# The low halves of a weight matrix: a subtraction on VectorE replaced by a negated copy on ScalarE and an adding DMA asked for by GpSimd

## The chip, the cores and the metric

The kernel runs on one core of a Trainium2 chip. The metric is the time of the device in microseconds (us), lower is better; a kernel is run several times and its median stands. Engines are called PE (TensorE, the matrix engine), DVE (VectorE), ACT (ScalarE), POOL (GpSimd) and SP (SyncE, which here only asks for DMAs).

## What is computed

Attention over 4 batches, 8 heads, 576 tokens and 64 dimensions a head, with a threshold on the scores; then two feed-forward networks over the 2304 tokens (model width 512). The change touches the first matrix of the second network, `w_in` of `_moe2_ref`, 512 by 2048:

```python
def _moe2_ref(x, w_in, w_out):
    h = x @ w_in
    g = np.maximum(h, 0.0) + np.log1p(np.exp(-np.abs(h)))
    return (g @ w_out).astype(np.float32)
```

The inputs are float64 for the weights and float32 for q, k, v. The products are made with pairs of float32r halves (below), so that they come close to float32.

## The kernel before, in words

**Products from halves.** A float32 value w is held as a high half, w rounded to float32r, and a low half, w minus the high half. A product of two such values takes three matmuls: high by high, high by low, low by high. So each weight matrix must be split before PE can use it, and `convert` does that.

**Stages.** The attention comes first, with units of the first network (`m1_unit`, 256 tokens each) between its heads. When the attention's buffers are closed (`close_at`), the weights of the second network are loaded and split while PE works on the last units of the first network, and the second network follows: token blocks 0, 1 and 4 as plain products, blocks 2 and 3 together by a scheme that trades products for sums.

**The split of w_in.** The matrix is loaded in 16 chunks of 128 by 512 float64 words (`prep_w2`), 512 KB each, into two rotating buffers of the tag `raw2`. Per chunk, `convert` issues: `a1` on ACT (the upper words, line 620), `a2` on DVE (the lower words shifted, line 621), `a4` on DVE (both joined to a float32 word, line 623), `a5` on ACT (rounded, the high half `w2h`, line 634) and a subtraction on DVE (the low half `w2l`, line 636). The buffer is free for the next load but one when the last of them is done. The same function splits the other matrices; its path for w_out of the second network (`raw_out`, `wo2h`, `wo2l`) is the same one.

**What reads it.** Block 0 of the second network (`m2_products`, line 809) multiplies chunk after chunk with the tokens in `x2m0h` and `x2m0l`, which SP loads from DRAM (`m2_load`, line 420). Its first product stands in the middle of the last units of the first network: their two matrix products (lines 697 and 751/752) and their transposes (line 734) share PE with it. Later blocks use the same halves again.

**What sets the order.** Each engine runs a list of operations that is written out by hand, `TURNS`, a table of operation numbers for each engine; negative numbers on PE are fillers, that many small matmuls on the identity (line 413), each in two passes in the trace. The costs that stand beside each `op(...)` served to make that table. An engine executes its list strictly in order, so a wait at the head holds everything behind it; SP asks for nearly all DMAs, in one list. POOL makes the identity at the start and then has nothing to do.

Of the kernel before, what the change touches and what calls it, by code (L numbers as in the profile page):

```python
# [9 lines left out]
F32 = mybir.dt.float32  # L10
F32R = mybir.dt.float32r
U32 = mybir.dt.uint32
# [58 lines left out]
def took(rows, row):  # L71
# [48 lines left out]
    "DVE":  # L120
# [267 lines left out]
def plan_of(nc, ctx, sb, const, ident, minus, pools, stacks, w1t, x2s, sums2, q, k, v, tau, w_in, w_out, g_ln, w2_in, w2_out, out):  # L388
# [221 lines left out]
    def convert(name, raw, hi, lo, n, after, view=lambda x: x, scale=None, turned=False):  # L610
# [3 lines left out]
        def lw():  # L614
            return view(raw.t[:, :, 0])

        def hw():
            return view(raw.t[:, :, 1])
# [525 lines left out]
```

## Time and profile before

| | before |
|---|---|
| time, median of 3 runs | 902.43 us (901.03 to 902.45) |
| the profiled execution's own time | 899.62 us |
| its span in the trace | 897.8 us |
| PE busy | 882.8 us, 98% |
| DVE busy | 722.0 us, 80% |
| ACT busy | 604.0 us, 67% |
| POOL busy | 0.7 us |
| DMA, share of 16 engines (hardware queue of SP) | 30.2%, 89.56 MB |

The time of an execution is a little longer than the span of its recorded instructions: here by 1.8 us. A busy PE is not PE at its peak, since matmuls overlap in the records; idle time of PE is what can be read from such a table, and what an engine off the path does with its idle time costs nothing by itself. All times in the sections below are of the profiled execution, counted from the start of its span.

### The profile page before, as it was taken

How to read it: one execution, taken by the hardware profiler on the slowest of the kernel's cores; microseconds unless marked ns; L12 is line 12 of the kernel's file. 1: busy time of each engine (PE TensorE's matmuls, PEld its weight loads, DVE VectorE, ACT ScalarE, POOL GpSimd, SP SyncE). 2: the span in 40 equal slices, each digit the busy share in tenths (PEclk: the TensorE clock that was granted, in tenths of full speed). 3: DMA queues.
4: the chain of work that ended last, by engine and by line, in shares of the span. 5: the costliest groups of instructions: out<-in, count | busy, mean ns of one | idle time of the engine just before them, and what ended most of it. 6: DMA issues, size and time to landing. Idle time of an engine off the chain costs nothing.

```text
span 897.8 us, 14490 instructions
## 1 busy us (share of the span) xinstructions
PE 882.8 (98%) x5348; PEld 693.9 (77%) x5348; DVE 722.0 (80%) x1558; ACT 604.0 (67%) x1189; POOL 0.7 (0%) x6
## 2 busy tenths in 40 slices
PE   7899999999999999999999999999999999999997
PEld 5567666777677777888888888888888988888886
DVE  5888988868878878778777979888998968999832
ACT  5989977887877788666666766755654645666521
POOL 0000000000000000000000000000000000000000
PEclk9999999999999999999999999999999999999999
DMA  8422300121113100083324444234337543212001
GB/s 278 171 94 57 106 7 1 56 85 54 46 53 89 42 13 2 24 279 132 106 95 141 164 134 169 99 127 152 120 133 236 181 164 129 70 71 71 34 15 47
DMA packets 46086, 90.86 MB, mean 101 GB/s; under 512 B 4800, under 2 KB 22720, under 8 KB 46016
## 3 DMA queue, kind: packets, MB, share of 16 engines
q1 hardware_dynamic: 45696, 89.56, 30.2%
q8 instruction: 42, 0.69, 0.3%
q10 hardware_dynamic: 320, 0.38, 0.2%
q14 instruction: 28, 0.23, 0.1%
HBM read 62.13 MB, written 27.79 MB: 100 GB/s over the span
## 4 chain that ended last, share of the span: by engine, by line
PE 93%; DVE 3%; ACT 2%; DMA 1%; issue 0%; SPq 0%; POOLq 0%; POOL 0%; ACTq 0%; DVEq 0%
PE w L842 21%; PE h L809 12%; PE w L697 11%; PE w L504 8%; PE s L528 8%; PE w L563 7%; PE w L751 7%; PE w L752 4%; PE h_b L1060 4%; PE h_a L1060 2%; PE h_g L1060 2%; PE w L734 2%; PE w L604 1%; PE s L583 1%; DVE nm L485 1%; PE w L542 1%
## 5 line engine op out<-in xcount | busy, mean ns | idle before, releaser
L485 DVE TENSOR_REDUCE nm<-s 128x1 f32<-128x576 f32 x144 | 103.2, 752 | 40.7 <-PE s L528 34.9
L842 PE MATMUL w<-wo2h,gh 128*128 128x512 f32 x288 | 112.3, 390 | 0.0
L842 PE MATMUL w<-wo2l,gh 128*128 128x512 f32 x288 | 112.3, 390 | 0.0
L842 PE MATMUL w<-wo2h,gl 128*128 128x512 f32 x288 | 112.0, 389 | 0.0
L486 ACT ACTIVATE E<-s,nm 128x576 f32<-128x576 f32 x128 | 92.6, 749 | 24.3 <-DVE nm L485 23.0
L488 DVE SCALAR_TENSOR_TENSOR E<-E,etau 128x576 f32<-128x576 f32 x128 | 101.9, 812 | 7.7 <-ACT E L486 5.3
L507 ACT COPY eT<-w 128x512 f32<-128x512 f32 (+1 forms) x186 | 94.2, 546 | 20.2 <-PE w L504 19.3
L751 PE MATMUL w<-lhl,wo1h 128*128 128x512 f32 x288 | 104.2, 401 | 0.0
L528 PE MATMUL s<-k,q 64*128 64x288 f32 x512 | 81.7, 429 | 3.5 <-ACT E L486 3.2
L504 PE MATMUL w<-ident,E 128*128 128x128 f32 x576 | 81.4, 280 | 1.7 <-ACT eT L507 0.9
L504 PEld LDWEIGHTS w<-ident,E 128*128 128x128 f32 x576 | 62.7, 140 | 24.4 <-ACT eT L507 7.3
L752 PE MATMUL w<-lhl,wo1l 128*128 128x256 f32 x288 | 80.6, 280 | 0.0
L563 PE MATMUL w<-eT,v 128*64 128x256 f32 (+1 forms) x680 | 76.3, 371 | 0.2
L528 PEld LDWEIGHTS s<-k,q 64*128 64x128 f32 x512 | 45.7, 186 | 26.1 <-ACT E L486 8.2
L563 PEld LDWEIGHTS w<-eT,v 128*64 128x64 f32 x680 | 44.7, 137 | 26.3 <-ACT eT L507 5.6
L751 PEld LDWEIGHTS w<-lhl,wo1h 128*128 128x128 f32 x288 | 54.1, 188 | 12.6 <-issue 0.4
L842 PEld LDWEIGHTS w<-wo2h,gl 128*128 128x128 f32 x288 | 54.1, 188 | 11.5
L842 PEld LDWEIGHTS w<-wo2h,gh 128*128 128x128 f32 x288 | 54.2, 188 | 10.1
L842 PEld LDWEIGHTS w<-wo2l,gh 128*128 128x128 f32 x288 | 54.2, 188 | 10.0
L697 PE MATMUL w<-w1h,xh 128*128 128x512 f32 x144 | 59.7, 415 | 0.0
L697 PE MATMUL w<-w1h,xl 128*128 128x512 f32 x144 | 56.5, 393 | 0.0
L697 PE MATMUL w<-w1l,xh 128*128 128x512 f32 x144 | 56.3, 391 | 0.0
(162 smaller groups left out, 1827.7 us busy)
## 6 DMA issues: line engine op xcount, KB each, us to landing
x2s<-x SPq DMA_DIRECT2D x36, 256.0 KB, 2.1
raw_in<-in_w_in_dram SPq DMA_DIRECT2D x16, 512.0 KB, 3.7
raw_out<-in_w_out_dram SPq DMA_DIRECT2D x16, 512.0 KB, 3.6
wsum<-g_w SPq DMA_DIRECT2D x16, 512.0 KB, 3.3
sw<-wsum SPq DMA_DIRECT2D x16, 512.0 KB, 3.7
v<-in_v_dram SPq DMA_DIRECT2D x16, 320.0 KB, 3.8
q<-in_q_dram SPq DMA_DIRECT2D x30, 144.0 KB, 3.2
raw<-in_w_out_dram SPq DMA_DIRECT2D x4, 1024.0 KB, 6.1
```

Source lines behind the costliest of these rows:

```text
L485: mx = op("DVE", 668, 750, lambda: dve.tensor_reduce(out=nm.t, in_=src(), axis=AX.XY, op=ALU.max, negate=True), after=[after], takes=[nm], ...
L486: ex = op("ACT", 638, 741, lambda: act.activation(out=dst().rearrange("p (a b) -> p a b", a=2), in_=src(), func=AF.Exp, bias=nm.t, scale=1.0),
L488: return op("DVE", 739, 900, lambda: dve.scalar_tensor_tensor(out=dst(), in0=dst(), scalar=etau, in1=dst(), op0=ALU.is_ge, op1=ALU.mult, a ...
L504: pe.transpose(bk.t[:, P * i:P * i + P], b_.t[:, c:c + P], ident)
L507: copies.append(op("ACT", occ, occ + 111, lambda: act.copy(out=eT.t[:, 0:width], in_=bk.t[:, 0:width]), after=[g], uses=[bk, eT]))
L528: pe.matmul(s[h].t[:, nh, 0:288], z["q"].t[r, c:c + P], z["k"].t[r, 288 * nh:288 * nh + 288], start=True, stop=True)
L563: pe.matmul(o_.t[64 * h:64 * h + 64, 0:W], z["v"].t[:, vcols(c, h)], e[8 if c == 8 else 4 * h + c](), start=(i == 0), stop=(i == 4))
L697: pe.matmul(ps.t, x__[:, part, :], w_[:, part, 512 * n:512 * n + 512], start=(part == 0 and j_ == 0), stop=(part == 3 and j_ == 2))
L751: pe.matmul(o.t.rearrange("p (a q) -> p a q", a=2), w1t["wo1h"][:, c, P * m:P * m + P], lhl.t[:, :, c, :], start=(c == 0), stop=False)
L752: pe.matmul(o.t[:, 0:256], w1t["wo1l"][:, c, P * m:P * m + P], lhl.t[:, 0, c, :], start=False, stop=(c == 7))
L809: pe.matmul(ps.t[:, 0:n], w2t["in", a, c][:, part, :], x(b_)[:, part, 0:n], start=(part == 0 and j_ == 0), stop=(part == 3 and j_ == 2))
L842: pe.matmul(ys[j].t, g_.t[:, P * j:P * j + P], w2t["out", a, c], start=(first and i == 0), stop=(last and i == 2))
```

## The change

For the 16 chunks of w_in alone (names that begin with `w2in`), the joined float32 words are written packed into the first half of the raw buffer, no longer into every second word; ACT writes minus the rounded words into the low half (`neg`, line 637 of the changed kernel), beside the high half as before; and a DMA that POOL asks for adds the float32 words of the raw buffer onto the low half, in place (line 638). The subtraction on DVE is gone. Readers of a low half now wait for that DMA, and so does the load that takes the raw buffer next. The table `TURNS` is written anew for all engines.

```diff
-        w_ = lambda: lw().bitcast(F32)
+        packed = name.startswith("w2in")
+        w_ = (lambda: raw.t.rearrange("p n t -> p (n t)")[:, 0:n].bitcast(F32)) if packed else lambda: lw().bitcast(F32)
...
-        a4 = op("DVE", 70 + 1068 * k_, 150 + 1070 * k_, lambda: dve.scalar_tensor_tensor(out=lw(), in0=hw(), scalar=3, in1=lw(), op0=ALU.logical_shift_left, op1=ALU.bitwise_or), after=[a1, a2], uses=[raw])
+        a4 = op("DVE", 70 + 1068 * k_, 150 + 1070 * k_, lambda: dve.scalar_tensor_tensor(out=w_().bitcast(U32), in0=hw(), scalar=3, in1=lw(), op0=ALU.logical_shift_left, op1=ALU.bitwise_or), after=[a1, a2], uses=[raw])
...
         a5 = op("ACT", 90 + 930 * k_, 200 + 940 * k_, lambda: act.copy(out=hi(), in_=w_()), after=[last], uses=[raw])
+        if packed:
+            neg = op("ACT", 90 + 930 * k_, 200 + 940 * k_, lambda: act.activation(out=lo(), in_=w_(), func=AF.Copy, scale=-1.0), after=[last], uses=[raw])
+            return [a5, op("POOL", 1100, None, lambda: pool.dma_start(out=lo(), in_=w_(), accum_op=ALU.add), after=[neg], uses=[raw], kb=2 * took(128, 4 * n))]
         if not turned:
             return [op("DVE", 70 + 1067 * k_, 150 + 1070 * k_, lambda: dve.tensor_tensor(out=lo(), in0=w_(), in1=f(hi()), op=ALU.subtract), after=[a5], uses=[raw])]
```

The table's row for POOL:

```diff
     "POOL":
-        "0",
+        "0 2303 2310 2317 2324 2331 2338 2352 2345 2359 2366 2373 2380 2387 2394 2401 2408",
```

**Order on SP** where the attention ends: `raw_in` are the loads of the chunks of w_in, `x2m0h` and `x2m0l` the loads of block 0's tokens (each in two parts), `x2s` the stores of the first network's results. Before:

```order
L420 DMA raw_in0_4644<-in_w2_in_dram 128x1024
L420 DMA raw_in1_4656<-in_w2_in_dram 128x1024
L420 DMA x2m0l_4662<-x2s0_87 128x4x256
L420 DMA x2s2_89<-x2_2_2_4423 128x512
L420 DMA x2m0l_4662<-x2s1_88 128x4x256
L420 DMA x2m0h_4674<-x2s0_87 128x4x256
L420 DMA raw_in2_4710<-in_w2_in_dram 128x1024
L420 DMA raw_in3_4734<-in_w2_in_dram 128x1024
L420 DMA x2m0h_4674<-x2s1_88 128x4x256
L420 DMA x2s3_90<-x2_3_0_4685 128x512
```

Now:

```order
L420 DMA raw_in0_4643<-in_w2_in_dram 128x1024
L420 DMA raw_in1_4647<-in_w2_in_dram 128x1024
L420 DMA x2m0h_4657<-x2s0_87 128x4x256
L420 DMA x2m0h_4657<-x2s1_88 128x4x256
L420 DMA x2s2_89<-x2_2_3_4437 128x512
L420 DMA x2s3_90<-x2_3_0_4650 128x512
L420 DMA raw_in2_4737<-in_w2_in_dram 128x1024
L420 DMA raw_in3_4749<-in_w2_in_dram 128x1024
L420 DMA x2m0l_4754<-x2s0_87 128x4x256
L420 DMA x2m0l_4754<-x2s1_88 128x4x256
```

Both parts of `x2m0l` have moved behind the loads of chunks 2 and 3; before, one part of `x2m0h` stood there.

**Order on ACT** at the same place, from the first step of chunk 0 to the first step of chunk 2 (in the changed kernel line 621 is `a1`, 635 the high half, 637 the negated copy; 700/704, 710/714, 754/758 and 758/762 are steps of the first network). Before:

```order
L620 ACTIVATE raw_in0_4644<-raw_in0_4644 128x512
L620 ACTIVATE raw_in1_4656<-raw_in1_4656 128x512
L634 CAST w2h0_4624<-raw_in0_4644 128x512
L700 COPY h4_1_4585<-w321_4584 128x512
L700 COPY h4_1_4585<-w322_4652 128x512
L634 CAST w2h1_4626<-raw_in1_4656 128x512
L754 COPY x2s_3_0_4730<-w315_4684 128x256
L710 ACTIVATE u4_1_4732,few4_1_4717<-h4_1_4585,few4_1_4717 128x1024
L758 CAST x2_3_0_4685<-x2s_3_0_4730 128x256
L620 ACTIVATE raw_in2_4710<-raw_in2_4710 128x512
```

Now:

```order
L621 ACTIVATE raw_in0_4643<-raw_in0_4643 128x512
L621 ACTIVATE raw_in1_4647<-raw_in1_4647 128x512
L637 ACTIVATE w2l0_4624<-raw_in0_4643 128x512
L635 CAST w2h0_4623<-raw_in0_4643 128x512
L637 ACTIVATE w2l1_4626<-raw_in1_4647 128x512
L758 COPY x2s_3_0_4705<-w315_4649 128x256
L704 COPY h4_1_4610<-w321_4609 128x512
L762 CAST x2_3_0_4650<-x2s_3_0_4705 128x256
L704 COPY h4_1_4610<-w322_4664 128x512
L635 CAST w2h1_4625<-raw_in1_4647 128x512
...
L621 ACTIVATE raw_in2_4737<-raw_in2_4737 128x512
```

The negated copies stand ahead of the high halves and ahead of the first network's steps.

**Order on PE** at block 0's first product, `h2_0_0` (line 809 before, 813 now); `w318` is the last group of sums of a unit of the first network, 16 matmuls in all. Before, its last rows and the product:

```order
L751 MATMUL w318_4826<-lhl3_4501,wo1h_85 128x512
L752 MATMUL w318_4826<-lhl3_4501,wo1l_86 128x256
L809 MATMUL h2_0_0_4854<-x2m0h_4674,w2h0_4624 128x512
L809 MATMUL h2_0_0_4854<-x2m0l_4662,w2h0_4624 128x512
L809 MATMUL h2_0_0_4854<-x2m0h_4674,w2l0_4625 128x512
```

Now:

```order
L701 MATMUL w332_4727<-w1h_83,xl5_0_4360 128x512
L813 MATMUL h2_0_0_4819<-x2m0h_4657,w2h0_4623 128x512
L813 MATMUL h2_0_0_4819<-x2m0l_4754,w2h0_4623 128x512
L813 MATMUL h2_0_0_4819<-x2m0h_4657,w2l0_4624 128x512
L755 MATMUL w318_4824<-lhl3_4495,wo1h_85 128x512
...
L813 MATMUL h2_0_1_4852<-x2m0h_4657,w2h1_4625 128x512
L813 MATMUL h2_0_1_4852<-x2m0l_4754,w2h1_4625 128x512
L813 MATMUL h2_0_1_4852<-x2m0h_4657,w2l1_4626 128x512
```

The first product has moved ahead of all 16 matmuls of `w318`, and the first product of chunk 1 now follows right behind them. No other operation has joined or left the work ahead of the first product. At the very start of PE's list the fillers are 15 (10 and 5) where they were 16 (15 and 1), and 2 further fillers some places later are gone.

## Rows read from the trace of the kernel before

**Rows 1.** The page: busy time of PE; its granted clock in 40 slices.

```profile
PE 882.8 (98%) x5348; PEld 693.9 (77%) x5348; DVE 722.0 (80%) x1558; ACT 604.0 (67%) x1189; POOL 0.7 (0%) x6
...
PEclk9999999999999999999999999999999999999999
```

**Rows 2.** Windows: start and end, length, then busy time of each engine.

```profile
core 0: us, PE busy (x) PEld busy (x) DVE busy (x) ACT busy (x) POOL busy (x), PEclk, DMA share, GB/s
0.00:36.00 36.00, 29.07 (x167) 19.66 (x168) 22.61 (x45) 26.30 (x46) 0.70 (x6) 1.00 0.86 279
36.00:380.00 344.00, 342.20 (x2706) 245.29 (x2706) 284.76 (x687) 279.80 (x567) 0.00 (x0) 1.00 0.16 48
380.00:525.00 145.00, 145.00 (x778) 122.64 (x775) 113.10 (x257) 94.59 (x199) 0.00 (x0) 1.00 0.44 151
640.00:700.00 60.00, 58.22 (x302) 49.79 (x301) 56.02 (x121) 32.02 (x65) 0.00 (x0) 1.00 0.56 183
```

**Rows 3.** Waits of PE, whole span: total us, times, longest.

```profile
PE s L528 <- ACT E L486: 3.2, 3, 1.6
PE h L809 <- DVE gw L826: 1.8, 1, 1.8
...
PE w L643 <- ACT eT L507: 1.2, 1, 1.2
```

**Rows 4.** Groups by line: the subtraction and the rounded copy of w_in's chunks.

```profile
L636 DVE TENSOR_TENSOR w2l<-raw_in,w2h 128x512 fp32r<-128x512 f32 x16 | 11.0, 686 | 1.0 <-ACT w2h L634 0.7
...
L634 ACT CAST w2h<-raw_in 128x512 fp32r<-128x512 f32 x16 | 10.5, 657 | 0.7 <-DVE raw_in L623 0.7
```

**Rows 5.** Timeline of the start: start us, duration us, engine, line, operation.

```profile
1.35 6.61 PE L413 MATMUL w<-ident 128*128 128x128 f32 x32 [1.35 <-POOL ident masks.py:199]
...
4.36 0.68 ACT L445 ACTIVATE k<-k 128x576 f32<-128x576 f32 x1 [1.10 <-DMA k<-in_k_dram]
...
7.89 1.24 PE L528 MATMUL s<-k,q 64*128 64x288 f32 x8
```

**Rows 6.** Timeline, SP alone, where the attention ends.

```profile
382.30 0.86 SPq L420 DMA_DIRECT2D raw_in<-in_w_in_dram  x2
...
389.69 2.38 SPq L420 DMA_DIRECT2D raw_in<-in_w_in_dram  x2
392.12 0.43 SPq L420 DMA_DIRECT2D x2m0h<-x2s  x1
```

**Rows 7.** Timeline: first steps of chunks 0 and 1 on ACT, joining of chunk 1 on DVE.

```profile
386.27 0.69 ACT L620 ACTIVATE raw_in<-raw_in 128x512 f32<-128x512 f32 x1 [2.48 <-DMA raw_in<-in_w_in_dram]
...
387.64 0.69 ACT L620 ACTIVATE raw_in<-raw_in 128x512 f32<-128x512 f32 x1 [0.68 <-DMA raw_in<-in_w_in_dram]
...
388.37 0.69 DVE L623 SCALAR_TENSOR_TENSOR raw_in<-raw_in 128x512 uint32<-128x512 uint32 x1 [0.29 <-ACT raw_in L620]
```

**Rows 8.** DMA issues by line: KB each, median us from issue to landing.

```profile
x2s<-x SPq DMA_DIRECT2D x36, 256.0 KB, 2.1
raw_in<-in_w_in_dram SPq DMA_DIRECT2D x16, 512.0 KB, 3.7
...
tsum<-g_x SPq DMA_DIRECT2D x12, 256.0 KB, 2.7
```

**Rows 9.** The tile x2m0h: time to landing of its two loads.

```profile
DMA to landing us min/median/max: 5.4/6.9/8.5
```

**Rows 10.** Timeline of PE: the first matmul of w318, and block 0's first product.

```profile
401.71 0.40 PE L751 MATMUL w<-lhl,wo1h 128*128 128x512 f32 x1
...
404.54 0.40 PE L809 MATMUL h<-x2m0h,w2h 128*128 128x512 f32 x1
```

**Rows 11.** Timeline around the longest later wait: ACT's wait, then PE's.

```profile
690.93 0.62 ACT L886 CAST g_w<-f_w 128x512 fp32r<-128x512 f32 x1 [3.13 <-DMA wsum<-g_w]
...
693.63 0.50 PE L809 MATMUL h<-x2m,w2h 128*128 128x256 f32 x2 [1.78 <-DVE gw L826]
```

**Rows 12.** Line 723: count, then duration ns min/median/max, first and last start.

```profile
L723 DVE TENSOR_SCALAR h<-u,few x18: 806/812/817, 109.2 to 506.1; 128x1024 f32<-128x1024 f32 x18
```

258 rows, old and new, of the table TURNS are left out of this document.

## The prediction

> **What bounds the kernel now.** Read the page first: PE is busy for 882.8 of 897.8 us, and its granted clock stays in the top tenth to the end [rows 1], which is the upper of its two levels, 2.4 GHz. So there is nothing to win from the clock, and at most 15.0 us from PE's idle time. Then ask where that idle time lies. The windows show it [rows 2]: 6.9 us of it in the first 36 us, 1.8 us between 36 and 380 us, 1.8 us between 640 and 700 us, and none at all between 380 and 525 us, the stretch in which the 16 chunks of w_in are split. There DVE works 113.1 and ACT 94.6 of 145 us; PE works all of it. The rest of the 15 us is the end of the span. PE's own waits tell what the idle time waited for [rows 3]: the largest is the start's loop of scores and softmax (3.2 us on ACT), the next a single wait of 1.8 us on DVE late in the second network. Neither is in the part that the change rewrites. The chain of work thus runs through PE's list from end to end, and a change pays only by what it does to that list and to the few waits at its head.
>
> **What goes.** 16 subtractions on DVE of 686 ns, 11.0 us in all [rows 4]. All are executed between 380 and 525 us, beside a PE without a gap: DVE falls there from 113.1 to about 102.1 of 145 us. Cover: PE's own work. Gain on the path: 0. The packed joining has as many elements as before, so I take `a4` at its old duration.
>
> **What comes on ACT.** 16 negated copies over the same 128x512 words as the rounded copy, 657 ns [rows 4]: 10.5 us, and ACT rises from 94.6 to about 105.1 of 145 us [rows 2]. Cover: again PE's work; ACT keeps 40 us of air in the stretch. On the path: 0, as long as ACT does not wait at the head of its list for a chunk that comes late, which is the next question.
>
> **What comes as a wait.** Each chunk now ends with an adding DMA, of which the trace shows no example. Call D the time from the end of the negated copy to its landing, POOL's asking included. It decides two things: when the low half can be read, and when the raw buffer is free for the next load but one. On POOL nothing stands behind it but the next such DMA.
>
> Bounds for D from the nearest rows [rows 8]: not under 2.1 us, the store of 256 KB, which reads and writes half of what the adding DMA reads; not over about 8.1 us, three passes of 256 KB one after another at 2.7 us. It reads 512 KB (source and destination), as many bytes as a raw load, 3.7 us, and writes 256 KB in addition. I take 4.5 us, between the raw load and two passes of 2.7 us.
>
> Follow chunks 0 and 1 in the changed order. Their loads start where they did, at 382.3 us [rows 6], since the attention's last matmul has kept its place but for one small exchange. ACT's first steps start at 386.3 and 387.6 us, and chunk 1 is joined by 388.37 + 0.69 = 389.1 us [rows 7]. On ACT follow the negated copy of chunk 0 (388.3 to 389.0), the rounded copy, and the negated copy of chunk 1 (389.6 to 390.3). The adding DMAs land at 389.0 + D and 390.3 + D: at 4.5 us, 393.5 and 394.8 us.
>
> *Readers.* Block 0's first product stood at 404.54 us and moves ahead of the 16 matmuls that began at 401.71 us [rows 10], to about 401.7 us: cover 8.2 us for low half 0. Chunk 1's first product comes 16 + 3 matmuls later, at about 405.2 us: cover 10.4 us. The other chunks' first products stand more than 120 groups of PE's work further on. No wait for a low half below D = 12.
>
> *The queue behind the buffer.* Here is the tight place. SP asks for the load of chunk 3 only once chunk 1's adding DMA has landed, and both loads of `x2m0l` are now queued behind it, where before only one load of `x2m0h` was. The first product needs `x2m0l`. The last of its two loads is asked for at about 390.3 + D + 0.9, three issues of some 0.4 us, as the one at 392.12 us took [rows 6]. Landing took 5.4 us for the load that stood in just this place, behind two raw loads, and 6.9 us in the median [rows 9]. So `x2m0l` is there at 396.6 + D to 398.1 + D, against PE's 401.7. PE waits nothing for D up to 5.1 (or 3.6) and one for one beyond. At 4.5 us: 0 to 0.9 us; I take 0.5.
>
> *ACT behind a late chunk.* The changed list puts 9 operations between the negated copy of chunk 1 and the first step of chunk 2. If chunk 2 lands late, ACT waits there; its 40 us of air and the free banks of PE's sums are the cover. I cost it at 0 for D near 4.5; without that cover each microsecond of D above costs one again at each pair of chunks.
>
> A page's price for D: the Trainium skill, "DMA: Bandwidth & Descriptors" (Anatomy of one DMA — SWDGE (gpsimd) path), gives a DMA asked for by GpSimd 2.0 us plus its bytes at 436 GB/s; for 512 KB that is an estimate of 3.2 us, and with it the wait for `x2m0l` would be 0 and the sum below -0.4. No row here shows such a DMA.
>
> **What is moved.** At the start one filler of 16 is gone, in the trace 2 of 32 passes: 6.61 / 32 = 0.21 us each [rows 5]. The first scores begin right behind the fillers, at 7.89 us, while k was scaled by 5.04 us, so the fillers hold them up: -0.4 us, if q has landed by 7.5. The 2 fillers further on stood in a gap: 0. The late wait of 1.8 us [rows 3] comes from ACT, which waits 3.13 us for a store of sums and holds DVE [rows 11]; the changed order on DVE still has that sum ahead of the operation that PE waits for, so I leave the wait where it is: 0, with bounds of -1.8 (gone) and +1.3 (ACT's whole wait passed on).
>
> **The sum.** -0.4 (filler) + 0.5 (`x2m0l`) + 0 = +0.1 us: 899.62 becomes 899.7. The profiled execution is 2.8 us under the median of the runs shown, 902.43; on that median the forecast is **902.5 us, no change**. What a measurement of this kernel can tell from no change is about 0.2%, 1.8 us. Own range of this case: D from 2.1 to 6 gives -0.4 to +2.0 us on the path, 902.0 to 904.4; with the late wait gone, 900.2.
>
> **Rivals.**
>
> *A, slower: the adding DMA is long.* Mechanism: SP's list waits for chunk 1's adding DMA, `x2m0l` behind it comes late, PE stands at block 0's first product. It decides from D = 5.1 (or 3.6) on, and passes +1.8 us of net loss at D = 7.3 (or 5.8). At D = 8.1 PE waits 3.0 to 4.5 us: net +2.6 to +4.1, **905.0 to 906.5 us**. For it: PE has no slack there and the load has moved behind the wait; nothing in the trace prices an adding DMA. Against: it would have to take twice a raw load of as many bytes read.
>
> *B, faster: the new order takes PE's waits away.* All lists are written anew, and the largest waits are 3.2, 1.8 and 1.2 us [rows 3]. With the late wait and half of the other two gone: -0.4 - 1.8 - 2.2 = -4.4, **898.0 us**; with the late wait alone, 900.2. For it: these waits are short and a few places on a list decide them. Against: the sums still stand ahead of DVE's step at the late wait, and the start is bound by the loop of scores, maximum and exponential, not by the order.
>
> *C, POOL held up by DVE.* What it would do here: while DVE runs one of its long operations that read and write at a raised rate, POOL can't prepare its DMA, so D grows by up to the length of that operation. The longest candidate is line 723, 1024 elements in 812 ns [rows 12]. D = 4.5 + 0.8 = 5.3 gives a wait of 0.2 to 1.7 us; with 1.0 the net is +0.6, **903.0 us**: inside "no change". The rule is the Trainium skill's, "SBUF — State Buffer" (Who interferes with whom): a DVE operation in a 2-port mode locks GpSimd out of a shared port for its whole length, and tensor_scalar is among those that can; the example of the same page (A bandwidth-pool intuition that's wrong (but worth ruling out)), 620 ns grown to 3100, would be an estimate of D = 7.0 and a net of about +2.2. No row here shows POOL asking for a DMA beside DVE.
>
> *D, a new wait elsewhere.* The same rewriting can open waits of a microsecond or two anywhere, above all between 640 and 700 us, where DVE has 4.0 us of air in 60 [rows 2]: +2 to +3, about 905.
>
> **How the numbers follow.** Forecast as summed, 0.33; C, which also stays within 0.2%, 0.11; A 0.19; D 0.11; B 0.26, of which the 900.2 variant has the larger part. Faster by over 0.2%: 0.26. Within: 0.44. Slower: 0.19 + 0.11 = 0.30. The range goes from 899.0, which takes in B with the late wait gone and leaves out its end at 898.0, to 906.5, the upper end of A: what lies outside are B's better half and a D beyond three passes, together under 0.2.
>
> **What would show it.** Right: DVE's time between 380 and 525 us falls by about 11 us and ACT's rises by 10.5, while PE still works all 145 us; POOL's 16 DMAs land in 3.7 to 5.4 us; block 0's first product starts at 401 to 403 us with a wait under 1 us; the first scores start near 7.5 us. Wrong: a wait of PE of over 2 us at the first product, or waits of ACT of several us at the chunks' first steps, speak for A; D in steps that go with DVE's line 723 for C; PE's late wait gone and the start's loop shorter, for B. If the split's stretch is as predicted and the time still differs by more than 1.8 us, then the rewritten order did it, not the adding DMA.

## The result, and the profile after

| | time, us | ratio to before, 95% interval |
|---|---|---|
| before | 902.43 (900.74 to 903.94) | |
| the change | 908.42 (906.81 to 912.27) | 1.0085 [1.0065, 1.0104] |

The change makes the kernel slower by 0.85%, some 7.7 us. The forecast was no change, 902.5 us; 908.42 lies outside its range and beyond Rival A's 906.5. The profiled execution took 907.60 us (span 905.7), so the two traces differ by 7.9 us of span, and that is what has to be found.

The page of the changed kernel, and its windows:

```profile
PE 884.7 (98%) x5342; PEld 694.4 (77%) x5342; DVE 712.2 (79%) x1542; ACT 610.8 (67%) x1205; POOL 15.2 (2%) x22
```

```profile
core 0: us, PE busy (x) PEld busy (x) DVE busy (x) ACT busy (x) POOL busy (x), PEclk, DMA share, GB/s
0.00:36.00 36.00, 28.25 (x142) 17.58 (x144) 21.76 (x42) 25.35 (x42) 0.69 (x6) 1.00 0.92 279
36.00:380.00 344.00, 341.70 (x2728) 246.79 (x2724) 285.42 (x689) 280.60 (x569) 0.00 (x0) 1.00 0.16 48
380.00:525.00 145.00, 138.76 (x727) 115.85 (x725) 98.49 (x233) 95.96 (x205) 13.61 (x15) 0.99 0.58 164
640.00:700.00 60.00, 60.00 (x295) 50.87 (x294) 56.98 (x117) 33.42 (x65) 0.00 (x0) 1.00 0.50 167
```

Against [rows 2]: PE, which worked all of 380 to 525 us, now idles there for 145 - 138.76 = 6.2 us, and its clock is not whole. It idles 0.8 us more at the start and 0.5 us more up to 380 us, and 1.8 us less between 640 and 700 us. Who waits, and for what, in 375 to 540 us of the changed kernel (columns: total us, times, longest; PE first, then ACT, DVE and SP's queue):

```profile
PE w L738 <- DVE h L727: 3.2, 2, 2.0
PE h L813 <- DMA x2m0l<-x2s: 1.9, 1, 1.9
PE w L701 <- DVE x2s L759: 0.8, 1, 0.8
...
ACT raw_in L621 <- DMA raw_in<-in_w_in_dram: 17.0, 9, 3.8
...
DVE raw_in L622 <- DMA raw_in<-in_w_in_dram: 11.4, 8, 2.3
...
SPq L420 <- DMA w2l<-raw_in: 25.4, 11, 8.8
```

The same rows of ACT, DVE and SP in the kernel before:

```profile
ACT raw_in L620 <- DMA raw_in<-in_w_in_dram: 6.1, 6, 2.5
...
DVE raw_in L621 <- DMA raw_in<-in_w_in_dram: 1.9, 4, 1.1
...
SPq L420 <- DVE w2l L636: 13.6, 7, 3.8
```

Read them from the bottom up. SP's loads stand 25.4 us in front of buffers that an adding DMA is the last to free; in the kernel before the subtraction was the last, and it was 13.6 us. The chunks land late, so ACT stands 17.0 us at their first steps instead of 6.1, and DVE 11.4 instead of 1.9. Of ACT's waits, 6.5 us stand at chunks 0 and 1, ahead of any adding DMA (3.2 in the kernel before [rows 7]); from chunk 2 on it is 10.5 us against 2.9. PE, which in the first network waits on what ACT and DVE have queued behind those steps, loses 3.2 + 0.8 us, and 1.9 at `x2m0l`. The longest of the first: DVE stands 2.1 us for chunk 8, until 437.0 us, the step that PE needs (line 727) comes behind it in DVE's list and ends at 439.6, and PE has stood 2.0 us for it. The adding DMA itself, in the views of its line and its issues:

```profile
L638 POOL DMA_DIRECT2D w2l<-raw_in x16: 859/859/1404, 390.2 to 529.0; - x16
...
DMA to landing us min/median/max: 3.3/3.8/6.4
```

and SP's timeline, to be held against [rows 6]:

```profile
381.69 1.20 SPq L420 DMA_DIRECT2D raw_in<-in_w_in_dram  x2
...
393.96 2.51 SPq L420 DMA_DIRECT2D raw_in<-in_w_in_dram  x2
396.52 0.98 SPq L420 DMA_DIRECT2D x2m0l<-x2s  x2
...
407.02 3.72 SPq L420 DMA_DIRECT2D raw_in<-in_w_in_dram  x2
...
418.83 2.82 SPq L420 DMA_DIRECT2D raw_in<-in_w_in_dram  x2
432.61 0.33 SPq L420 DMA_DIRECT2D raw_in<-in_w_in_dram  x1
```

The pairs of chunks are loaded at 381.7, 394.0, 407.0, 418.8 and 432.6 us: one pair each 50.9 / 4 = 12.7 us, counted from the first load of a pair.

Last, the clock. PE's first product starts, then waits for `x2m0l`; behind the wait matmuls of this shape take up to 0.63 us instead of 0.40, until 408.7 us:

```profile
402.20 0.39 PE L813 MATMUL h<-x2m0h,w2h 128*128 128x512 f32 x1
404.52 0.47 PE L813 MATMUL h<-x2m0l,w2h 128*128 128x512 f32 x1 [1.93 <-DMA x2m0l<-x2s]
...
406.23 0.63 PE L755 MATMUL w<-lhl,wo1h 128*128 128x512 f32 x1
...
408.70 0.40 PE L755 MATMUL w<-lhl,wo1h 128*128 128x512 f32 x1
```

```profile
400.00:404.00 4.00, 2.59 (x12) 1.80 (x10) 2.15 (x5) 2.21 (x5) 0.94 (x2) 1.00 0.79 261
404.00:408.00 4.00, 3.48 (x12) 2.94 (x13) 1.58 (x2) 3.23 (x7) 1.33 (x2) 0.65 0.79 135
408.00:412.00 4.00, 4.00 (x24) 3.45 (x23) 2.30 (x5) 2.92 (x6) 0.00 (x0) 0.93 0.55 156
```

After PE had stood for 1.9 us the clock fell to the lower of its two levels, 1.2 GHz: between 405.2 and 408.5 us it is granted at 0.50. With a mean of 0.65 and 0.93 the lost clock is 4 x 0.35 + 4 x 0.07 = 1.7 us, which the busy time hides. The account: 6.2 + 1.7 + 0.8 + 0.5 - 1.8 = 7.4 of the 7.9 us.

### The profile page after: what moved, and what is told of

Read it like the earlier page. It is cut to its first block, busy times and chain, and to the rows that moved or that the text cites. A ratio compares the mean times of both kernels' runs of the same rounds, so it can differ in the third digit from the quotient of the medians.

```text
span 905.7 us, 14567 instructions
## 1 busy us (share of the span) xinstructions
PE 884.7 (98%) x5342; PEld 694.4 (77%) x5342; DVE 712.2 (79%) x1542; ACT 610.8 (67%) x1205; POOL 15.2 (2%) x22
## 4 chain that ended last, share of the span: by engine, by line
PE 86%; DMA 6%; ACT 3%; DVE 1%; issue 1%; SPq 1%; POOL 0%; POOLq 0%; ACTq 0%
PE w L846 22%; PE h L813 12%; PE w L701 8%; PE w L504 8%; PE w L563 7%; PE s L528 7%; PE w L755 6%; PE h_b L1064 4%; PE w L756 3%; PE h_a L1064 2%; PE h_g L1064 2%; DMA raw_in<-in_w_in_dram 2%; DMA w2l<-raw_in 2%; PE w L738 1%; DMA v<-in_v_dram 1%
```

## The experiments

Theory 1: the raw buffer, held until the adding DMA has landed, delays the loads, and the late chunks cost the time. Theory 2: the rewritten order, or ACT's added work, costs it. Each ratio is against runs of the kernel before on the same chip; their medians were 901.29 us for the first four kernels, 900.29 for the next four and 900.04 for the last four. Lists of operations and edits are shown in part, cut at `...` or at the end of a line.

**1. new_way_old_order.** The change's low halves under the lists of the kernel before (numbers are those of the changed kernel; 2302 is the negated copy of chunk 0):

```diff
 "ACT":
-2305 2301 1802 1807
+2305 2302 2301 1802 1807
 "POOL":
-0
+0 2303 2310 2317 2324 2331 ...
```

> The change's low halves (negated copy, adding DMA) put into the order of the kernel before: each negated copy stands right ahead of the high half on ACT, the subtractions are gone from DVE, everything else is in the old order. Theory 1 (the raw buffer, held until the adding DMA has landed, is what costs): 907 to 911 us, with ACT waiting for raw_in for over 12 us in 375-540 (6.1 us before) and PE waiting there for a late thing; the wait of 1.8 us near 693 stays, and the start is that of before (its PE losses some 1.5 us under the change's). Theory 2 (the rewritten order is what costs, not the DMA): 901.5 to 903 us, and no new PE wait in 380-525.

Measured: 928.12 us, 1.0292 [1.0270, 1.0314]. Far beyond both.

```profile
SPq L420 <- DMA w2l<-raw_in: 57.3, 12, 10.5
...
PE w L738 <- DVE h L727: 9.6, 2, 4.9
PE w L701 <- DVE x2s L759: 7.5, 2, 6.6
```

(SP's queue and PE, 375 to 540 us.) The new way costs 26.8 us under the old order. In the profiled execution PE idles 12.4 us between 380 and 525 us and loses 8.7 more to a mean clock of 0.94. Its first 36 us lose 4.8 more than those of the kernel before, 1.6 in idle time and 3.2 at a clock of 0.91; these lie ahead of every adding DMA, so they are not its price.

**2. old_way_new_order.** The subtraction of before under the change's order; the high half takes the negated copy's place (numbers of the kernel before):

```diff
 "ACT":
-2304 2301 1802 1807 2307 1737
+2304 2301 2307 1737 1802 1739
```

> The subtraction of before (DVE, from the buffer) under the change's order: the high half takes the place of the negated copy on ACT, the subtraction follows it on DVE. Theory 1 (held buffer): the 8.8 us that PE loses in 375-450 are gone and the start (+1.5) and the late wait (-2) of the new order stay: 899.5 to 903 us. Theory 2 (the order): 907 to 910 us, with PE waits of over 3 us in 380-450.

Measured: 899.16 us, 0.9977 [0.9965, 0.9989]; a little below the range of Theory 1, nowhere near that of Theory 2. With the order alone the kernel is faster by 0.2%. Runs 1 and 2 with the two kernels make a square of four: old way 1.0 and 0.9977, new way 1.0292 and 1.0085, under the old and the new order. The new way costs 2.9% under the old order and, 1.0085 against 0.9977, 1.1% under the new, some 9.7 us: the rewriting takes most of the price away and leaves the rest.

**3. late_half_first.** One edit to the change, on SP:

```diff
-2297 2304 2662 2664 1666 1741 2311 2318 2663 2665 1750
+2297 2304 2662 2664 1666 1741 2663 2665 2311 2318 1750
```

> The change with one edit: on SP the two loads of x2m0l are asked for ahead of the raw loads of chunks 2 and 3, which wait for the adding DMAs. Theory 1 (queue behind the held buffer): x2m0l lands before 395, the wait of 1.9 us at 402 and the stretch at half clock behind it (1.6 us) go: 904.3 to 905.5 us. Rival: PE, now earlier, waits as long for the low halves of the next chunks, which are as late as before: 907 to 909 us.

Measured: 907.48 us, 1.0076 [1.0055, 1.0096], not to be told from the change. The wait for `x2m0l` is gone, and others have its place (PE, 375 to 540 us):

```profile
PE w L701 <- DVE x2s L759: 3.6, 2, 2.8
PE w L738 <- DVE h L727: 2.7, 1, 2.7
```

and in the windows around the first of them:

```profile
408.00:412.00 4.00, 1.35 (x7) 0.88 (x7) 2.65 (x4) 3.04 (x7) 0.00 (x0) 1.00 0.89 229
412.00:416.00 4.00, 3.81 (x10) 3.06 (x11) 2.48 (x7) 1.89 (x4) 0.00 (x0) 0.57 0.25 97
```

The rival's time holds, though by another link than it named: PE doesn't wait for low halves. Earlier by the wait it was spared, it stands some seven microseconds further on for a sum whose steps ACT and DVE have queued behind the late chunks (they stand 4.2 and 3.7 us for chunk 2, until 401.8 us), and the clock falls behind that wait instead (0.57). The load in the tight place was not the cause by itself, only the first to show it. (`x2m0l` was asked for at 393.3 us, behind a store on SP, and landed some 6 us later, not before 395 as expected, but before PE asked.)

**4. no_adding.** The change without the adding DMA; the low half holds only minus the rounded words:

```diff
-op("POOL", 1100, None, lambda: pool.dma_start(out=lo(), in_=w_(), accum_op=ALU.add), after=[neg], uses=[raw], ...)
+op("POOL", 1100, None, lambda: None, after=[neg], uses=[raw], ...)
```

> The change without the adding DMA: the low half holds only minus the rounded words, and the buffer is free when the two copies are done. Order, copies and all else as in the change. Theory 1 (held buffer): raw loads 2 and 3 are asked for 4 to 5 us earlier, ACT's waits for raw_in in 375-540 fall from 17 us to under 6, PE loses under 2 us in 375-450: 899.5 to 902.5 us. Theory 2 (the order, or ACT's 10.5 us more work): 907 to 909 us.

Measured: 898.19 us, 0.9974 [0.9960, 0.9989], a little under the range of Theory 1. ACT's waits, 8.8 us, are above the 6 expected, but 6.4 of them stand at chunks 0 and 1. SP's queue, ACT and PE, 375 to 540 us, and SP's timeline:

```profile
SPq L420 <- ACT w2h L635: 7.9, 5, 4.9
...
ACT raw_in L621 <- DMA raw_in<-in_w_in_dram: 8.8, 5, 3.8
...
PE w L701 <- DVE x2s L759: 0.4, 2, 0.3
```

```profile
379.62 1.20 SPq L420 DMA_DIRECT2D raw_in<-in_w_in_dram  x2
...
390.82 0.87 SPq L420 DMA_DIRECT2D raw_in<-in_w_in_dram  x2
...
401.55 1.34 SPq L420 DMA_DIRECT2D raw_in<-in_w_in_dram  x2
411.10 0.87 SPq L420 DMA_DIRECT2D raw_in<-in_w_in_dram  x2
421.48 0.42 SPq L420 DMA_DIRECT2D raw_in<-in_w_in_dram  x1
```

A pair each 41.9 / 4 = 10.5 us, against 12.7. Counted from the first load, the change's pairs are later by 1.1, 3.4, 5.7 and 9.1 us, and the two ratios lie 1.1% apart, about 10 us. Beside old_way_new_order (0.9977) this is also the answer on the work moved: DVE without its 11 us of subtractions and ACT with 10 us more of copies is worth nothing that can be measured.

**5. four_buffers.** The change, with buffers for chunks 2, 3, 6 and 7 lent by the space of the weights of chunks 10 and 11:

```diff
+        if which == "in" and c in (2, 3, 6, 7):
+            raw = Buf("w2a", f"lent{c % 2}", lambda: pools["w2a"].tile([P, 512, 2], U32, tag=f"w2{'hl'[c % 2]}10", name=f"raw_{which}{c}"))
...
```

> The change with two more raw buffers for chunks 2, 3, 6 and 7, lent by the space of the weights of chunks 10 and 11, which are written only after 470 us; the order is unchanged. An adding DMA then holds a buffer that the chunk two later does not need. Theory 1 (held buffer): raw loads 2 and 3 go before 386, ACT's waits for raw_in in 375-540 fall from 17 to under 8 us, x2m0l is there before PE asks, clock 1.0: 898 to 901.5 us. Rival (what costs is that the low halves themselves come late, or ACT's 10.5 us more, or the traffic of the adding DMAs): 905 to 908.5 us.

Measured: 898.62 us, 0.9987 [0.9974, 0.9999]. SP's queue, ACT and PE, 375 to 540 us:

```profile
SPq L420 <- DMA w2l<-raw_in: 5.0, 3, 4.3
...
ACT raw_in L621 <- DMA raw_in<-in_w_in_dram: 5.7, 5, 2.1
...
PE w L701 <- DVE x2s L759: 0.8, 1, 0.8
PE w L738 <- ACT lhl L744: 0.2, 1, 0.2
```

All 16 adding DMAs run, at the same places of the same order, and the 0.85% is gone. So neither the low halves' lateness nor ACT's copies nor the transfers' traffic cost it; the holding of the buffer did. (Chunks 2 and 3 are asked for at 389.8 us, behind a store on SP, and not before 386 as expected. Chunk 0 is loaded at 378.1 us here, some 1.5 us ahead of no_adding and 3.6 ahead of the change; that part isn't separated here, but run 12 loads it as early and gains nothing.)

**6. add_twice.** Each adding DMA asked for twice; the low half then holds the word too much:

```diff
-lambda: pool.dma_start(out=lo(), in_=w_(), accum_op=ALU.add)
+lambda: [pool.dma_start(out=lo(), in_=w_(), accum_op=ALU.add) for _ in range(2)]
```

> The change with each adding DMA asked for twice, one after the other (the low half then holds the word too much): only the time from the negated copy to the buffer's release grows. Theory 1: it grows from 4.8 to some 6 to 9 us, and by the 10.2 us that 4.8 us cost (908.4 against 898.2 without the adding DMA), 2.1 us per us, the time is 911 to 917 us. Rival (one late transfer behind the first chunks, then slack again): 907.5 to 910 us.

Measured: 947.88 us, 1.0526 [1.0506, 1.0546]: the direction of Theory 1, and a slope far above its own. SP's queue, POOL and PE, 375 to 540 us, and two of SP's loads:

```profile
SPq L420 <- DMA w2l<-raw_in: 66.2, 13, 11.5
...
POOL w2l L638 <- DMA w2l<-raw_in: 47.0, 14, 4.8
...
PE w L738 <- DVE h L727: 17.3, 3, 8.1
PE h L813 <- DMA x2m0l<-x2s: 7.7, 1, 7.7
```

```profile
380.57 1.20 SPq L420 DMA_DIRECT2D raw_in<-in_w_in_dram  x2
...
451.71 0.33 SPq L420 DMA_DIRECT2D raw_in<-in_w_in_dram  x1
```

and a window:

```profile
408.00:412.00 4.00, 2.63 (x7) 2.24 (x8) 1.55 (x2) 3.23 (x7) 1.06 (x3) 0.50 0.60 148
```

The second request waits on POOL for the first to land, and the next chunk's requests wait behind it, so the hold grew by more than I had reckoned: 7.9 us for chunk 0 and 12.0 for chunk 1. Loads 0 to 8 take 71.1 us, a pair each 17.8. From no_adding to the change the period grows by 2.2 us and the kernel by about 10; from there to here by 5.1 and by about 40, in idle time of PE (26 us between 380 and 525) and in clock (0.91 there, some 13 us). The other runs stand in the same row. At 9.1 us a pair (the kernel before), 10.5 (no_adding), 10.6 (old_way_new_order) and 11.0 (four_buffers) nothing is lost; at 12.0 (two_lent, run 9) the ratio is 1.0014, at 12.7 (the change) 1.0085, at 13.7 (new_way_old_order, under the other order) 1.0292, at 17.8 here 1.0526. So up to some 11 us the period is covered, and beyond that the time climbs with it. Late work of PE holds the loads back in its turn, so the row alone doesn't show which drives which; four_buffers does.

**7 and 8. old_way_late_order, old_way_order_380.** The kernel before with the change's order after 525 and after 380 us. My seam rule put ACT's table load, operation 2, behind the seam:

```diff
 "ACT":
-"4 6 2 7 9 113 116 ...
+"4 6-7 9 113 116 ...
```

> The kernel before, with its own order for all that started before 525 us and the change's order for the rest. If the 0.23% that the change's order gained with the subtraction of before is the late wait near 693 us alone: 899 to 900.7 us, with that wait of 1.8 us gone. If it is gained in 375-525 or in the attention part: 901 to 902 us.

> The kernel before, with its own order for all that started before 380 us and the change's order after that. If the start is better in the old order (PE lost 1.5 us less in 0-50 in the profile of before than in that of the change): 897 to 898.7 us, under the 899.2 of the old way in the new order throughout. If the start's difference was chance of one execution: 899 to 900 us.

Measured: 949.13 us, 1.0548 [1.0526, 1.0569], and 925.15 us, 1.0269 [1.0245, 1.0293]. They answer another question than was asked. ACT's groups of the first hold 45 table loads (one fewer than I wrote for run 10), 18 of them at the logarithm of `m1_unit` and 16 more at its exponential (line 720):

```profile
L719 ACT ACT_TABLE_LOAD x18 | 23.1, 1283 | 0.3
```

where the kernel before has one. So with the common set's load behind the seam, the earlier part pays 1.28 us again and again where the function changes. Nothing about the order follows from these two.

**9. two_lent.** As four_buffers, with `c in (2, 3)`:

```diff
-        if which == "in" and c in (2, 3, 6, 7):
+        if which == "in" and c in (2, 3):
```

> As four_buffers, but only chunks 2 and 3 have a lent buffer; 6 and 7 wait for the buffers of 4 and 5 again. Theory 1a (each held buffer costs where it stands: in the change 3.8 us at 402 with the half clock, then 1.3, 2.1 and 1.0 at 417, 437 and 440): the first goes, the others stay: 902.5 to 905 us. Theory 1b (the first late pair delays all the rest): 898 to 900.5 us, and ACT's waits for raw_in are under 9 us.

Measured: 901.55 us, 1.0014 [1.0000, 1.0028], between the two. SP's queue and PE, 375 to 540 us:

```profile
SPq L420 <- DMA w2l<-raw_in: 10.1, 6, 4.3
...
PE w L738 <- DVE h L727: 2.3, 1, 2.3
PE w L701 <- DVE x2s L759: 0.8, 1, 0.8
```

Of the 0.98% between the change and four_buffers, freeing the first pair gives back 0.71%, 6.4 us and so more than the 3.6 (1.9 of wait, 1.7 of clock) that stand at its own place: the first delay is carried on; and 6 and 7, held again, cost 0.27% (the two intervals only just part), with a wait of 2.3 us and a clock of 0.57 behind it (436 to 440 us). Of the two pairs freed here both pay, and the first more. The pairs after them, held in four_buffers too, cost nothing that shows.

**10 and 11. old_way_late_order_2, old_way_order_380_2.** Runs 7 and 8 with the table load left at its place; after 380 us, for instance:

```diff
 "ACT":
-2304 2301 1802 1807 2307 1737 1809
+2304 2301 2307 1737 1802 1739 1807
```

> The kernel before with the change's order after 525 us only, ACT's first table load left at its old place (in old_way_late_order it had gone to the seam, and 46 table loads of 1.28 us took the place of one). If the change's order gains by the late wait alone: 898.5 to 900.2 us where before has 900.3 to 901.3. If it gains in 375-525 or not at all: 900.3 to 902 us.

> The kernel before with the change's order after 380 us only, the table load in its old place. If the start of the old order is better: 897 to 898.4 us. If the start's difference was chance: within 0.1% of old_way_new_order, 0.9977 of before, 898.4 to 899.8 us.

Measured: 899.53 us, 0.9994 [0.9982, 1.0006]; and 901.75 us, 1.0017 [1.0007, 1.0027]. In the first the late wait is gone, PE works all 60 us between 640 and 700; its ratio is too near 1 to tell a gain of 0.2% from none. The second fits neither expectation. Its PE is busy for 26.01 us of the first 36, against 29.07 [rows 2] and 28.35 in the first, and up to 380 us the three run the same lists. So the first 36 us differ by up to 3 us for a reason that isn't the order; which it is stays open. (Its profiled execution is the slowest of its eleven.) Such a difference, 0.3% of the span, is more than the 0.2% that run 2 gained, so neither run tells where that gain came from, or that it is the order's.

**12. old_way_four_buffers.** old_way_new_order with the lent buffers (edit as in 5):

```diff
+        if which == "in" and c in (2, 3, 6, 7):
```

> old_way_new_order (the subtraction of before under the change's order) with the four raw buffers. With no adding DMA nothing is held that PE waits for, so the lent buffers should be worth nothing: 0.9965 to 0.999 of before. A rival: the 0.2 to 0.8 us that PE still loses in 375-450 go, 0.9950 to 0.9965.

Measured: 899.12 us, 0.9991 [0.9982, 0.9999]. More buffers are worth nothing where no adding DMA holds one, and nor is the early load of chunk 0, at 377.8 us against 380.8 in old_way_new_order. Of the versions that compute the whole result the fastest by its ratio is old_way_new_order, 0.9977, though its interval overlaps with those of this run and of four_buffers: faster than the kernel before by 0.2%, and than the change by about 1.1%.

## Why the prediction was wrong, point by point

- **DVE and ACT, at no gain and no cost: right.** DVE's total falls by 722.0 - 712.2 = 9.8 us; the negated copies took 0.64 us each in the mean, 10.2 in all. no_adding against old_way_new_order shows that the exchange is worth nothing on the path. The forecast's own sign, DVE's and ACT's time between 380 and 525 us, shows neither: DVE falls there by 14.6 us and ACT rises by 1.4, since work moved across the edges of that stretch (ACT has 6 operations more in it, not 16).
- **D, taken at 4.5 us: right in the mean.** The negated copy of chunk 0 ends at 389.85 us, POOL asks at 390.16, and SP loads chunk 2 at 393.96: 4.1. For chunk 1 it is 390.89 to 396.1: 5.2. Over chunks 0 to 7 it is 3.6 to 6.8, 4.8 in the mean; the longest is chunk 3's. The estimate of 3.2 us that the Trainium skill gave, "DMA: Bandwidth & Descriptors" (Anatomy of one DMA — SWDGE (gpsimd) path), lies below all eight, and just below the shortest landing, 3.3 us. (With it the forecast's own sum is -0.4, not below it.)
- **Low halves in time for their readers: right.** PE waits for no `w2l` in 375 to 540 us.
- **The queue behind the buffer: mechanism right, term mis-sized.** 0.5 us was taken, 1.9 measured. The negated copy of chunk 1 ended 0.6 us later than reckoned, its D was 5.2 for 4.5, and the last load of `x2m0l`, asked for at 397.0 us, took 7.4 us to land where 5.4 to 6.9 were taken; PE came to the product 0.5 us later than reckoned, which gave that much back. What I didn't see is that the wait has a second price, 1.7 us at the lower clock.
- **"ACT behind a late chunk", costed at 0: this is the step that failed.** ACT waited 17.0 us for chunks, not 6.1, DVE 11.4, not 1.9, and PE 4.0 us behind them. I followed chunks 0 and 1 and their load, and set ACT's 40 us of air over the whole stretch against the rest. But two buffers are a ring, and a part of D is added to every turn of it: against no_adding a pair takes 12.7 us for 10.5. (Not the whole of D: there the high half's copy, which comes later on ACT, is what frees the buffer.) The lateness grows from pair to pair, while ACT and DVE hold work for PE in the same lists. I had written down what happens without that cover and never asked whether a mean of air is one. four_buffers shows that the held buffers carry the loss, late_half_first that it isn't the load of `x2m0l` alone, and two_lent that a part of the first pair's price is paid further on.
- **The start, -0.4 us: not shown.** The scores begin at 7.01 us instead of 7.89, but under the old order alone the profiled executions range from 6.63 (new_way_old_order) to 7.89.
- **The late wait, left in place: wrong.** It is gone (640 to 700 us), as in Rival B, and the new order with the old subtraction is faster by 0.2%. In the account it takes 1.8 us off the loss.
- **Rival A** had the sign and the first link, and stopped at it: 906.5 us was its end for a D of 8.1, where 3.6 to 6.8 gave 908.4. **Rival C**: most requests took POOL 0.86 us whatever DVE did. Three ran beside line 727: two took 1.4 us, as the rule of the Trainium skill ("SBUF — State Buffer", Who interferes with whom) would have it, and the third 0.86. That is 0.5 us for each of the two, and four_buffers, with as many requests, loses nothing. **Rival D**: the new waits opened in the split's stretch, not between 640 and 700 us, where PE waits for nothing.
- **"If the split's stretch is as predicted ... the order did it"**: the stretch was not, PE lost 6.2 us in it, and the square of runs 1 and 2 clears the order: under the old one the new way costs more still.

## What to carry to other kernels

A transfer that is the last to read a rotating buffer lengthens each turn of the rotation, not one step: compute the period of the ring before and after, and compare it with the rate at which its consumer needs the turns. Air that an engine has on the mean of a stretch is no cover for a wait at the head of its list, when the same list holds work that the bottleneck needs. When moving one late load leaves the time as it was, look for the cause upstream: lend another buffer, or leave the transfer out, and see.

## What was not expected of the hardware

- PE can pay for a wait twice. In the change, after 1.9 us without work, the granted clock was half for some 3.4 us; in late_half_first it followed the new wait, 2.8 us, to its new place (0.57 in 412 to 416 us); in two_lent it followed one of 2.3 us; in add_twice, around a wait of 7.7 us, it was down to 0.50 in 408 to 412 us. Not every wait does it: in the change PE idles 2.0 us between 436 and 440 us, and the clock stays at 1.00 to 448. What decides between the two isn't shown.
- An adding DMA of 256 KB, from the raw buffer onto the low half, landed in 3.8 us in the median (3.3 to 6.4), a little less than a raw load of 512 KB (4.1 in the same trace).
- 45 table loads of 1.28 us where one load of a common set, moved 525 us later, did not stand ahead of the work.
